# Linear attention and a GEGLU feed-forward on one core: both weight halves in one tile, one norm on two engines, one sum of h placed later

## The chip, the core and the metric

The kernel runs on one core of a Trainium2 chip. A core has TensorE (PE, matmuls), VectorE (DVE), ScalarE (ACT), GpSimd (POOL) and a queue (SP) that issues DMAs. Each engine works through its own instructions in the order in which the program lists them, and engines wait for each other on semaphores. The metric is the device time of one execution in microseconds; lower is better.

## The reference

Eight batches of 576 tokens with 8 heads of 64. The attention is linear: queries are normalized over the head dimension, keys over the tokens. Its output, 4608 tokens by 512, goes through a gated feed-forward of width 1536.

```python
q_s = np.exp(q - max(q, -1)); q_s = q_s / (sum(q_s, -1) + 1e-09)
k_s = np.exp(k - max(k, 2));  k_s = k_s / (sum(k_s, 2) + 1e-09)
kv = np.einsum('bhsd,bhse->bhde', k_s, v)
attn = np.einsum('bhsd,bhde->bhse', q_s, kv)
x = attn.transpose(0, 2, 1, 3).reshape(B * S, H * D)
out = (gelu(x @ w_gate) * (x @ w_val)) @ w_out
```

Inputs and output are float32; the kernel works in float16 with float32 sums.

## The kernel before

**Batches.** The loop at L1023 goes over batches 0 to 6, then 8, then 7. Batches 0 to 7 are the 512 main tokens of each batch; "batch 8" gathers the remaining 64 tokens of all eight. While the feed-forward of one batch runs on TensorE, the attention of the next is prepared: `exp` (L208, ScalarE), `norm_sum` (L226, VectorE: row sums and reciprocal), `norm_mul` (L248, VectorE or GpSimd: the exponentials, called eq, times the reciprocals), a transpose (`unit_t` on TensorE in batches 0 and 1, `unit_td` by DMA later), `unit_kv` and `unit_x`, which gives xt, the input of the feed-forward.

**Feed-forward.** Its width is cut into 12 tiles of 128 (fi). Batches 0 and 1 take each tile with plain matmuls into psg and psv (L467), then Gelu on ScalarE (L472) and the product on VectorE (L473), which gives ht. Batches 2 and later use a Winograd form of Strassen's scheme: 7 block products in place of 8. For that they need sums of blocks:

- sums of the weights: `sum_wgv` (L591), four for gate (g) and four for value (v), on pairs of tiles k and k+3. Sum 1 is a21+a22, sum 2 is sum 1 - a11, sum 3 is a11-a21 written over a21 in the weight tile itself, sum 4 is a12 - sum 2. For k = 0 to 2 they are made in batch 0, three k in one operation; for k = 6, 7, 8 each k by itself, and gate and value each by itself: 128x256 elements an operation. Where these results lie is set by `w_sum` (L586), `wst16` (L553) and the views `ws` at L121 to L123.
- sums of x: `sum_x` (L600), on GpSimd.
- sums of h for the output product: `sum_h` (L572), four for each pair of tiles: sums 1 and 2 on VectorE, 3 and 4 mostly on GpSimd in batches 2 and 3. `sum_w` (L558) makes the sums of w_out.

**Order.** It is written by hand. In batches 2 and later the strings at L621 to L626 list the steps: "k.i" is step i of the pair k (`pair_step`), "8g" and "8v" are plain halves of tile 8 (`half`), and other words stand for work planned under that name. FOUR serves batches 2 and 3. Its "s1" plans the first and third sum of h of pair 1 (tiles 1 and 4, with 7 and 10), "u1" the second and fourth; "u1" is called in the output stage. In step 3 of a pair, `upper` (L660) makes the upper half of ht: Gelu on ScalarE, then a product on GpSimd (L663).

The table `plan`, filled by `at(b, kind, i, ...)`, hangs other work onto the places of the program: FI after a tile of batches 0 and 1, NS in the output stage. The last norm of batch 1 (head pair 3) hangs at (0, NS, 16) at L948 and runs on VectorE; the next place, (0, NS, 17), has sum_w(3) and sum_w(2) on GpSimd. The transposes that need the norm are the first thing in batch 1 (L953, `unit_t`).

**Output stage.** `out_strassen` (L742) runs product 1 (psa), 2 (psb), 5 (psc), 6 (psa), 3 (psc), 7 (psa) and 4 (psa), six tiles each. In between, VectorE or ScalarE takes snapshots (L762, L764) of psa and psc, and VectorE adds bank and snapshot into the output tile yo (L770). Product 3 adds into psc and so comes after psc's snapshot; product 4 overwrites psa and so comes after the add of psa. The place (b, NS, 2) lies between psa's second snapshot and that add.

Of the kernel before, what the change touches and what calls it, by code (L numbers as in the profile page):

```python
# [9 lines left out]
f32 = mybir.dt.float32  # L10
f16 = mybir.dt.float16
ACTF = mybir.ActivationFunctionType
ALU = mybir.AluOpType
# [5 lines left out]
def kernel(  # L19
# [10 lines left out]
    nc = tc.nc  # L30

    B, H, S, D = q.shape
    C = H * D
    F = moe_w_gate.shape[1]
    P = 128
    HP = H // 2
# [12 lines left out]
    NO = NFI // 2  # L49

    const = ctx.enter_context(tc.tile_pool(name="const", bufs=1))
    wpool = ctx.enter_context(tc.tile_pool(name="wpool", bufs=1))
# [52 lines left out]
    ek_b, eq_b, v16_b = [], [], []  # L105
# [7 lines left out]
    ws = {(nm, 0): const.tile([P, 3, 2, NO // 2 * P], f16, name=f"ws{nm}") for nm in "gv"}  # L113
# [4 lines left out]


    kt1 = ld_b["k"][1].rearrange("p h x -> p (h x)").bitcast(f16)  # L120
    for i, nm in enumerate("gv"):  # L121
        n = 3 * NO * P
        ws[(nm, 1)] = kt1[:, i * n:(i + 1) * n].rearrange("p (s c f) -> p s c f", s=3, c=2)  # L123
    cc_b = [x.rearrange("p n c -> p (n c)").bitcast(f32)[:, 0:1024].rearrange(
        "p (i t r) -> p i t r", i=2, t=2) for x in eq_b]

# [1 line left out]
        "p (i c r) -> p i c r", i=4, c=2)]  # L128

    q0r = [x[0:64].rearrange("p (h d) -> p h d", d=D) for x in (  # L130
        kt1[:, 2 * n:].bitcast(f32), eq_b[1].rearrange("p n c -> p (n c)").bitcast(f32)[:, 1024:])]

    def buf(bs, b):
        return bs[b % len(bs) if b < 4 else 0]
# [10 lines left out]
    nc.gpsimd.memset(v16_b[0][:, :, :, D:D + 1], 1.0)  # L145
    nc.gpsimd.memset(ld_b["k"][1][:, :, 0:D], -1e30)

    wg_sb = wpool.tile([P, HP, F], f16, name="wg_sb")
    wv_sb = wpool.tile([P, HP, F], f16, name="wv_sb")
    wo_sb = wpool.tile([P, NFI, C], f16, name="wo_sb")  # L150


# [82 lines left out]
    def norm_pair(b, g, n0, engs):  # L235

        n = NC - n0
        e = buf(eq_b, b)[:, n0:NC, 2 * g * P:(2 * g + 2) * P].rearrange("p n (h d) -> p n h d", d=D)
        rq = att.tile([P, n, 4], f32, name="rq2", tag="rq2", bufs=2)
        nc.vector.reduce_sum(rq, e, axis=mybir.AxisListType.X)  # L240
        rrq = att.tile([P, n, 4], f32, name="rrq2", tag="rrq2", bufs=2)
        nc.vector.reciprocal(out=rrq, in_=rq)  # L242
        for j in range(2):
            st[(b, "norm", 2 * g + j)] = (e[:, :, 2 * j:2 * j + 2], rrq[:, :, 2 * j:2 * j + 2], n)
        for j, eng in enumerate(engs):
            norm_mul(b, 2 * g + j, eng)

    def norm_mul(b, hp, eng="dve"):  # L248
        e, rrq, n = st[(b, "norm", hp)]
        (nc.gpsimd if eng == "pool" else nc.vector).tensor_tensor(  # L250
            out=e, in0=e, in1=rrq.unsqueeze(-1).to_broadcast((P, n, 2, D)), op=ALU.mult)

    def norm(b, hp, eng="dve", n0=0):
        norm_sum(b, hp, n0)
        norm_mul(b, hp, eng)
# [21 lines left out]
    st = {}  # L277
# [272 lines left out]
    tw, ws67 = {}, {}  # L550


    def wst16(name, key):  # L553
        t = wstp.tile([P, NO * 256 + 512], f16, name=name, tag="wst")
        ws67[key] = t[:, NO * 256:].rearrange("p (c f) -> p c f", c=2)
        return t[:, 0:NO * 256].rearrange("p (j c) -> p j c", j=NO)

    def sum_w(i, eng="dve"):  # L558
        t = wst16(f"tw{i}", (None, ("g", 0), ("v", 0), ("g", 1), ("v", 1))[i])
        b11, b12 = wo_sb[:, 0:NO, 0:256], wo_sb[:, 0:NO, 256:512]  # L560
        b21, b22 = wo_sb[:, NO:NFI, 0:256], wo_sb[:, NO:NFI, 256:512]
        a, b = {1: (b12, b11), 2: (b22, tw.get(1)), 3: (b22, b12), 4: (b21, tw.get(2))}[i]
        (nc.gpsimd if eng == "pool" else nc.vector).tensor_tensor(out=t, in0=a, in1=b, op=ALU.subtract)
        tw[i] = t

    sh = {}

    def make_s():
        for i in (1, 2):
            sh[i] = wst16(f"sh{i}", (None, ("g", 2), ("v", 2))[i])  # L570

    def sum_h(j0, j1, which, eng="dve"):  # L572
        step = 1 if j0 in (0, 4) and j1 < NO + (j0 > 0) else NO // 2
# [9 lines left out]

    def w_sum(nm, j, k, n=1):  # L586
        if k in (NO, NO + 1):
            return ws67[(nm, j)][:, :, (k - NO) * P:(k - NO + n) * P]
        return ws[(nm, k // NO)][:, j, :, k % NO * P:(k % NO + n) * P]

    def sum_wgv(nm, i, k=0, n=NO // 2, eng="dve"):  # L591
        w = wg_sb if nm == "g" else wv_sb
        lo, hi = slice(k * P, (k + n) * P), slice((k + NO // 2) * P, (k + NO // 2 + n) * P)
        a11, a21, a12, a22 = w[:, 0:2, lo], w[:, 0:2, hi], w[:, 2:4, lo], w[:, 2:4, hi]
        t = [w_sum(nm, j, k, n) for j in range(3)]
        o, a, b, op = {1: (t[0], a21, a22, ALU.add), 2: (t[1], t[0], a11, ALU.subtract),
                       3: (a21, a11, a21, ALU.subtract), 4: (t[2], a12, t[1], ALU.subtract)}[i]
        (nc.gpsimd if eng == "pool" else nc.vector).tensor_tensor(out=o, in0=a, in1=b, op=op)  # L598
# [7 lines left out]
    def product_gv(i, ps, xt, k, first):  # L606
        lo, hi = slice(k * P, (k + 1) * P), slice((k + NO // 2) * P, (k + NO // 2 + 1) * P)
        xs = xs_b[xt is st.get((B - 1, "xt"))]
        for t, w, nm in ((0, wv_sb, "v"), (1, wg_sb, "g")):
            for c in range(2):  # L610
                a = {1: w[:, c, lo], 2: w[:, 2 + c, lo], 4: w[:, 2 + c, hi], 7: w[:, c, hi]}.get(i)
                if a is None:
                    a = w_sum(nm, {3: 2, 5: 0, 6: 1}[i], k)[:, c]
                x = {1: xt[:, c, 0:256], 2: xt[:, 2 + c, 0:256], 3: xt[:, 2 + c, 256:512],
                     4: xs[:, 3, c], 5: xs[:, 0, c], 6: xs[:, 1, c], 7: xs[:, 2, c]}[i]
                nc.tensor.matmul(ps[:, t], a, x, start=(first and t == 0 and c == 0), stop=(c == 1),  # L616
                                 skip_group_check=True)
# [1 line left out]


    FOUR = ("a 7g l 7v n 0.1 6.1 0.2 6.2 0.3 6.3 m p 10g 0.4 6.4 1.1 t 10v 1.2 s0 8g u0 1.3 8v 1.4 2.1"  # L621
            " 11g s1 2.2 11v 2.3")
    FIVE = ("a 8g l 8v n m 0.1 6.1 0.2 6.2 0.3 6.3 0.4 1.1 p 6.4 7.1 t 1.2 7.2 1.3 s0 7.3 2.1 1.4 u0 11g 2.2"
            " y 7.4 11v 2.3 s1")
    SIX = ("0.1 6.1 0.2 6.2 0.3 6.3 0.4 1.1 6.4 7.1 s0 1.2 7.2 1.3 u0 7.3 1.4 2.1 7.4 8.1 2.2"
# [306 lines left out]
    FI, NS, PR = range(3)  # L932
    plan = {}

    def at(b, kind, i, *fns):
        plan.setdefault((b, kind, i), []).extend(fns)

    L = lambda f, *a: (lambda: f(*a))

    def load_2nd():  # L940
        load_batch(2, ((q, "q"), (k, "k")))

    at(0, FI, NFI - 1, L(exp, "q", 1, 0, 4), L(exp, "q", 1, 4, 8), load_2nd, L(exp, "k", 1, 0, 4),
       L(cast_w_o, 3), L(cast_w_o, 4), L(cast_w_o, 5),
       L(norm, 1, 0), L(norm, 1, 1), L(norm_sum, 1, 2), L(norm_mul, 1, 2, "pool"),
       L(cast_v, 1, 0, 4, "act"), L(exp, "k", 1, 4, 8))
    at(0, NS, 5, L(unit_t, 1, 0))
    at(0, NS, 16, L(unit_kv, 1, 0), L(cast_v, 1, 4, 8), L(load_batch, 2, ((v, "v"),)),  # L948
       L(norm, 1, 3))
    at(0, NS, 17, L(unit_x, 1, 0, "act", True), L(unit_x, 1, 1, "act", True), L(sum_w, 3, "pool"),  # L950
       L(sum_w, 2, "pool"))
    at(0, NS, 7, L(exp, "q", 2))
    first1 = [[L(unit_t, 1, 1), L(unit_kv, 1, 1)],  # L953
# [10 lines left out]
    at(1, FI, 2, L(unit_trem, 1))  # L964
    at(1, FI, 3, L(norm, 2, 2, "pool"), L(load_batch, 3, ((q, "q"), (k, "k"))))
    at(1, FI, 4, L(exp, "k", 2, 0, 4), L(norm, 2, 3, "pool"), L(sum_w, 4), make_s)
    at(1, FI, 5, L(cast_v, 2, 0, H))
    at(1, FI, 8, L(unit_td, 2))
# [5 lines left out]
    for i, x in enumerate(("g1", "v1", "g2", "v2", "g4", "v4")):  # L974
        at(0, FI, 5 + i, L(sum_wgv, x[0], int(x[1])))
    at(0, FI, NFI - 2, L(sum_w, 1))
    at(1, NS, 1, L(sum_wgv, "g", 3))
    at(1, NS, 2, L(sum_wgv, "v", 3))
    for b in range(2, B):
        n = b + 1  # L980
# [14 lines left out]
    for b in range(2, B - 1):  # L995
        n = b + 1
# [6 lines left out]
    for b in range(2, B + 1):  # L1003
        for j in range(NO // 2 - 1):
# [3 lines left out]
            else:  # L1008
                at(b, PR, f"s{j}", L(sum_h, j, NO, (3,), "pool"))
                at(b, PR, f"u{j}", L(sum_h, j, NO, (2,)), L(sum_h, j, NO, (4,), "pool"))  # L1010
    for b, i, kind, dk, xs_ in (
            (1, 6, FI, 0, ("g1", "v1", "g2", "v2", "g4", "v4")), (1, 9, FI, 0, ("g3", "v3")),
            (2, 1, NS, 1, ("g1", "v1", "g2", "v2")), (3, 2, NS, 1, ("g4", "v4", "g3", "v3")),
            (4, 2, NS, 2, ("g1", "v1", "g2", "v2")), (6, 1, NS, 2, ("g4", "v4")), (6, 2, NS, 2, ("g3", "v3"))):
        for x in xs_:
            at(b, kind, i, L(sum_wgv, x[0], int(x[1]), NO + dk, 1, "pool" if b < 3 else "dve"))


    def ride(b, kind, i):
# [3 lines left out]
    for b in order:  # L1023
# [16 lines left out]
        if b == 0:  # L1040
# [5 lines left out]
            for ns in range(4):  # L1046
                cut = 9 if ns == 2 else 7 if ns == 3 else NFI
# [37 lines left out]
```

## Time and profile before

| What | us |
|---|---|
| median of 3 runs | 294.36 (294.34 to 294.36) |
| the profiled execution | 298.55 |
| its span, first to last instruction | 296.8 |

Busy time in that execution:

| Engine | us |
|---|---|
| PE | 282.7 |
| DVE | 232.5 |
| POOL | 200.0 |
| ACT | 198.4 |

The mean granted TensorE clock is 0.991 of full speed. The lines of the profile in the prediction give a start in us from the span's first instruction, a length in us, the engine, the line of the code, the operation, "out<-in" by the program's names with shapes, and a count; a bracket at the end is the engine's idle time just before, with what ended it. Lines that stand for several instructions ("x4") are merged.

### The profile page before, as it was taken

The numbers are of one execution on the slowest core, as the hardware profiler recorded it, in microseconds if no ns is written. First come the engines' busy times: TensorE is split into PE (matmuls) and PEld (weight loads), VectorE is DVE, ScalarE is ACT, GpSimd is POOL, SyncE is SP. The second block draws the span as 40 slices with busy tenths as digits, with TensorE's granted clock in tenths as the row PEclk, the third lists the DMA queues.
The fourth block names the chain that finished last, engine by engine and source line by source line (L and its number), as shares of the span: only waits on it lengthen the run. The fifth ranks groups of instructions, "written<-read, shape, count | busy, mean of one in ns | idle before, by whom it ended". The sixth has DMA issues, their size and how long they took to land.

```text
span 296.8 us, 6506 instructions
## 1 busy us (share of the span) xinstructions
PE 282.7 (95%) x2497; PEld 208.5 (70%) x2497; DVE 232.5 (78%) x432; ACT 198.4 (67%) x332; POOL 200.0 (67%) x189
## 2 busy tenths in 40 slices
PE   3899997999999999999899999999999999999994
PEld 1444444544877686868688877888788888888883
DVE  2855889786997787768997989887988879938982
ACT  3763377374788669866977697769775477537650
POOL 1567548469278869995797589668976476293640
PEclk9999999799999999999999999999999999999998
DMA  6999999978119901990099208930332110033003
GB/s 222 372 380 390 400 390 393 342 282 190 58 75 353 285 3 71 331 301 9 23 328 334 44 3 305 334 71 2 141 58 45 71 74 0 3 71 73 2 0 141
DMA packets 54622, 51.72 MB, mean 174 GB/s; under 512 B 18496, under 2 KB 50496, under 8 KB 54592
## 3 DMA queue, kind: packets, MB, share of 16 engines
q1 hardware_dynamic: 52864, 49.49, 51.8%
q10 hardware_dynamic: 1728, 1.84, 1.9%
q8 instruction: 19, 0.31, 0.4%
q14 instruction: 11, 0.09, 0.1%
HBM read 37.75 MB, written 9.44 MB: 159 GB/s over the span
## 4 chain that ended last, share of the span: by engine, by line
PE 88%; DVE 6%; DMA 2%; issue 1%; ACT 1%; POOL 1%; POOLq 0%; ACTq 0%
PE pga L616 21%; PE psa L732 14%; PE psg L467 11%; PE psv L467 11%; PE pgc L616 10%; PE psc L732 6%; PE pgb L616 5%; PE psb L732 4%; PE psy L535 3%; DMA qt<-in_q_dram 2%; PE pskv L343 2%; DVE eq L250 1%; DVE kt L598 1%; PE pst L368 1%; PE psx L430 1%
## 5 line engine op out<-in xcount | busy, mean ns | idle before, releaser
L250 POOL TENSOR_TENSOR eq<-eq,rrq 128x640 f16<-128x640 f16 (+1 forms) x27 | 34.7, 1303 | 16.6 <-DVE rrq L242 8.4
L732 PEld LDWEIGHTS <-ht 128*128 128x128 f16 x384 | 36.8, 98 | 8.8 <-issue 4.0
L467 PE MATMUL psg<-xt,wg_sb 128*128 128x512 f16 x152 | 41.6, 383 | 0.0
L467 PE MATMUL psv<-xt,wv_sb 128*128 128x512 f16 x152 | 41.4, 382 | 0.0
L663 POOL TENSOR_TENSOR ht<-eq 128x512 f16<-128x512 f32 x17 | 21.6, 1273 | 19.2 <-ACT eq L661 19.2
L616 PEld LDWEIGHTS <-wv_sb 128*128 128x128 f16 x280 | 27.0, 98 | 8.0 <-issue 0.8
L616 PEld LDWEIGHTS <-wg_sb 128*128 128x128 f16 x280 | 27.4, 98 | 3.2
L582 POOL TENSOR_TENSOR s<-ht,sh 128x512 f16<-128x512 f16 x16 | 18.7, 1169 | 14.5 <-DVE sh L582 14.5
L472 ACT ACTIVATE gl<-psg 128x512 f32<-128x512 f32 x24 | 13.8, 597 | 21.2 <-PE psg L467 21.2
L643 ACT ACTIVATE glq<-pgb 128x256 f32<-128x256 f32 x35 | 13.3, 381 | 21.1 <-PE pgb L616 14.4
L644 DVE SCALAR_TENSOR_TENSOR ht<-pga,glq 128x256 f16<-128x256 f32 x35 | 14.8, 422 | 14.9 <-ACT glq L643 14.6
L467 PEld LDWEIGHTS <-wv_sb 128*128 128x128 f16 x152 | 14.9, 98 | 16.3 <-issue 1.2
L582 POOL TENSOR_TENSOR ht<-ht 128x512 f16<-128x512 f16 x16 | 19.0, 1188 | 10.0 <-DVE sh L582 10.0
L467 PEld LDWEIGHTS <-wg_sb 128*128 128x128 f16 x152 | 15.0, 99 | 14.8 <-issue 0.6
L732 PE MATMUL psa<-tw,ht 128*128 128x256 f16 x192 | 23.4, 272 | 1.6 <-DVE yo L770 1.5
L673 ACT COPY pgb<-pga 128x512 f32<-128x512 f32 x35 | 20.4, 582 | 6.1 <-PE pga L616 5.8
L473 DVE SCALAR_TENSOR_TENSOR ht<-psv,gl 128x512 f16<-128x512 f32 x24 | 16.0, 685 | 9.3 <-PE psv L467 7.3
L653 ACT ACTIVATE snq<-pga 128x512 f32<-128x512 f32 x35 | 20.9, 600 | 3.5 <-PE pga L616 3.2
L188 POOL CAST v<-vt 128x640 f16<-128x640 f32 x26 | 18.7, 760 | 6.7 <-PE pskv L343 5.4
L663 POOL TENSOR_TENSOR ht<-cc 128x512 f16<-128x512 f32 x16 | 20.3, 1271 | 3.0 <-ACT cc L661 3.0
L616 PE MATMUL pga<-xs,wv_sb 128*128 128x256 f16 x116 | 22.1, 272 | 0.2 <-DVE cc L657 0.2
L212 ACT ACTIVATE ek<-kt 128x1280 f16<-128x1280 f32 (+1 forms) x11 | 19.1, 1748 | 4.8 <-DMA kt<-in_k_dram 3.3
(182 smaller groups left out, 761.9 us busy)
## 6 DMA issues: line engine op xcount, KB each, us to landing
out_dram<-yo SPq DMA_DIRECT2D x15, 512.0 KB, 3.4
kt<-in_k_dram SPq DMA_DIRECT2D x7, 640.0 KB, 8.3
vt<-in_v_dram SPq DMA_DIRECT2D x7, 640.0 KB, 5.5
qt<-in_q_dram SPq DMA_DIRECT2D x7, 640.0 KB, 6.7
qt<-in_q_dram SPq DMA_DIRECT2D x8, 512.0 KB, 7.1
wost<-in_moe_w_out_dram SPq DMA_DIRECT2D x6, 512.0 KB, 7.9
kt<-in_k_dram SPq DMA_DIRECT2D x6, 512.0 KB, 9.2
vt<-in_v_dram SPq DMA_DIRECT2D x6, 512.0 KB, 6.0
```

Of the source, the lines that this page charges most:

```text
L188: nc.gpsimd.tensor_copy(out=dst, in_=src)
L212: nc.scalar.activation(out=dst[:, n0:NC, h0 * D:h1 * D].rearrange(o, d=D, **({"t": 2} if b >= QUAD else {})), in_=heads(tiles[(nm, b)], b, ...
L250: (nc.gpsimd if eng == "pool" else nc.vector).tensor_tensor(out=e, in0=e, in1=rrq.unsqueeze(-1).to_broadcast((P, n, 2, D)), op=ALU.mult)
L467: nc.tensor.matmul(ps, w[:, ci, fi * P:(fi + 1) * P], xt[:, ci, :], start=(ci == 0), stop=(ci == HP - 1))
L473: nc.vector.scalar_tensor_tensor(out=ht[:, fi, :], in0=psv, scalar=_H_SCALE, in1=gl, op0=ALU.mult, op1=ALU.mult)
L582: (nc.gpsimd if eng == "pool" else nc.vector).tensor_tensor(out=o, in0=a, in1=b, op=op)
L616: nc.tensor.matmul(ps[:, t], a, x, start=(first and t == 0 and c == 0), stop=(c == 1), skip_group_check=True)
L644: nc.vector.scalar_tensor_tensor(out=ht[:, fi, 0:256], in0=ps[:, 0], scalar=_H_SCALE, in1=gl, op0=ALU.mult, op1=ALU.mult)
L653: nc.scalar.activation(out=sn, in_=ps, func=ACTF.Copy, scale=_H_SCALE)
L663: (nc.vector if k == NFI - NO // 2 - 1 else nc.gpsimd).tensor_tensor(out=ht[:, k:k + NO // 2 + 1:NO // 2, 256:512], in0=cc[:, :, 0], in1=c ...
L673: nc.scalar.copy(out=pb, in_=pa)
L732: nc.tensor.matmul(ps[t], a, w, start=(first and j == js[0] and (t == ts[0] or ps[t].tensor is not ps[ts[0]].tensor)), stop=(j == js[-1]), ...
```

## The change

Four edits:

1. The weights of gate and value lie in one tile, wgv_sb, instead of two; wg_sb and wv_sb are views of its halves.
2. For k = 6, 7, 8 a sum is made for both weights by one operation (`sum_w1`) of 128x512 elements. The results lie with gate and value side by side: in `ws67` for k = 6, 7 and in `ws8`, a view of the second key buffer, for k = 8. The places in the plan stay the same: GpSimd in batches 1 and 2, VectorE in batches 3, 4 and 6.
3. The last norm of batch 1 is multiplied on two engines: rows 0 to 2 of 5 on VectorE, rows 3 and 4 on GpSimd.
4. In FOUR, "s1" moves from behind "11g" to the end of the list, behind "2.3".

```diff
-    for i, nm in enumerate("gv"):
-        n = 3 * NO * P
-        ws[(nm, 1)] = kt1[:, i * n:(i + 1) * n].rearrange("p (s c f) -> p s c f", s=3, c=2)
+    ws8 = kt1[:, 0:12 * P].rearrange("p (s w c f) -> p s w c f", s=3, w=2, c=2)
...
-    wg_sb = wpool.tile([P, HP, F], f16, name="wg_sb")
-    wv_sb = wpool.tile([P, HP, F], f16, name="wv_sb")
+    wgv_sb = wpool.tile([P, 2, HP, F], f16, name="wgv_sb")
+    wg_sb, wv_sb = wgv_sb[:, 0], wgv_sb[:, 1]
...
+    def norm_mul2(b, hp, cut):
+        e, rrq, n = st[(b, "norm", hp)]
+        for eng, r in ((nc.vector, slice(0, cut)), (nc.gpsimd, slice(cut, n))):
+            eng.tensor_tensor(out=e[:, r], in0=e[:, r], in1=rrq[:, r].unsqueeze(-1).to_broadcast(
+                (P, r.stop - r.start, 2, D)), op=ALU.mult)
...
-        ws67[key] = t[:, NO * 256:].rearrange("p (c f) -> p c f", c=2)
+        ws67[key] = t[:, NO * 256:].rearrange("p (w c f) -> p w c f", w=2, c=2)
...
-        t = wst16(f"tw{i}", (None, ("g", 0), ("v", 0), ("g", 1), ("v", 1))[i])
+        t = wst16(f"tw{i}", (None, (NO, 0), (NO, 1), (NO, 2), (NO + 1, 0))[i])
...
+    def sum_w1(i, k, eng):
+        lo, hi = slice(k * P, (k + 1) * P), slice((k + NO // 2) * P, (k + NO // 2 + 1) * P)
+        a11, a21, a12 = wgv_sb[:, :, 0:2, lo], wgv_sb[:, :, 0:2, hi], wgv_sb[:, :, 2:4, lo]
+        a22 = wgv_sb[:, :, 2:4, hi]
+        t = [ws8[:, j] if k == NO + 2 else ws67[(k, j)] for j in range(3)]
         o, a, b, op = {1: (t[0], a21, a22, ALU.add), 2: (t[1], t[0], a11, ALU.subtract),
                        3: (a21, a11, a21, ALU.subtract), 4: (t[2], a12, t[1], ALU.subtract)}[i]
         (nc.gpsimd if eng == "pool" else nc.vector).tensor_tensor(out=o, in0=a, in1=b, op=op)
...
-            " 11g s1 2.2 11v 2.3")
+            " 11g 2.2 11v 2.3 s1")
...
-       L(norm, 1, 3))
+       L(norm_sum, 1, 3), L(norm_mul2, 1, 3, 3))
...
-    for b, i, kind, dk, xs_ in (
-            (1, 6, FI, 0, ("g1", "v1", "g2", "v2", "g4", "v4")), (1, 9, FI, 0, ("g3", "v3")),
-            (2, 1, NS, 1, ("g1", "v1", "g2", "v2")), (3, 2, NS, 1, ("g4", "v4", "g3", "v3")),
-            (4, 2, NS, 2, ("g1", "v1", "g2", "v2")), (6, 1, NS, 2, ("g4", "v4")), (6, 2, NS, 2, ("g3", "v3"))):
-        for x in xs_:
-            at(b, kind, i, L(sum_wgv, x[0], int(x[1]), NO + dk, 1, "pool" if b < 3 else "dve"))
+    for b, kind, i, dk, x in ((1, FI, 6, 0, 1), (1, FI, 6, 0, 2), (1, FI, 6, 0, 4), (1, FI, 9, 0, 3),
+                              (2, NS, 1, 1, 1), (2, NS, 1, 1, 2), (3, NS, 2, 1, 4), (3, NS, 2, 1, 3),
+                              (4, NS, 2, 2, 1), (4, NS, 2, 2, 2), (6, NS, 1, 2, 4), (6, NS, 2, 2, 3)):
+        at(b, kind, i, L(sum_w1, x, NO + dk, "pool" if b < 3 else "dve"))
```

More of the change, by code (lines that the diff above doesn't have):

```diff
@@ L130 @@
     q0r = [x[0:64].rearrange("p (h d) -> p h d", d=D) for x in (
-        kt1[:, 2 * n:].bitcast(f32), eq_b[1].rearrange("p n c -> p (n c)").bitcast(f32)[:, 1024:])]
+        kt1[:, 36 * P:].bitcast(f32), eq_b[1].rearrange("p n c -> p (n c)").bitcast(f32)[:, 1024:])]
     def buf(bs, b):
@@ L569, in make_s @@
         for i in (1, 2):
-            sh[i] = wst16(f"sh{i}", (None, ("g", 2), ("v", 2))[i])
+            sh[i] = wst16(f"sh{i}", (None, (NO + 1, 1), (NO + 1, 2))[i])
     def sum_h(j0, j1, which, eng="dve"):
@@ L582, in sum_h, with w_sum @@
             (nc.gpsimd if eng == "pool" else nc.vector).tensor_tensor(out=o, in0=a, in1=b, op=op)
[L586 to L589, printed above, removed]
+    def w_sum(nm, j, k):
+        if k < NO:
+            return ws[(nm, 0)][:, j, :, k * P:(k + 1) * P]
+        return (ws8[:, j] if k == NO + 2 else ws67[(k, j)])[:, "gv".index(nm)]
     def sum_wgv(nm, i, k=0, n=NO // 2, eng="dve"):
@@ L594, in sum_wgv @@
         a11, a21, a12, a22 = w[:, 0:2, lo], w[:, 0:2, hi], w[:, 2:4, lo], w[:, 2:4, hi]
-        t = [w_sum(nm, j, k, n) for j in range(3)]
+        t = [ws[(nm, 0)][:, j, :, k * P:(k + n) * P] for j in range(3)]
+        o, a, b, op = {1: (t[0], a21, a22, ALU.add), 2: (t[1], t[0], a11, ALU.subtract),
+                       3: (a21, a11, a21, ALU.subtract), 4: (t[2], a12, t[1], ALU.subtract)}[i]
+        (nc.gpsimd if eng == "pool" else nc.vector).tensor_tensor(out=o, in0=a, in1=b, op=op)
+    def sum_w1(i, k, eng):
[3 more added lines that the diff above has]
+        t = [ws8[:, j] if k == NO + 2 else ws67[(k, j)] for j in range(3)]
         o, a, b, op = {1: (t[0], a21, a22, ALU.add), 2: (t[1], t[0], a11, ALU.subtract),
```

## The prediction

> **What bounds the kernel now.** I read the page first, then the waits of TensorE, then the timeline around each wait.
>
> ```profile
> PE 282.7 (95%) x2497; PEld 208.5 (70%) x2497; DVE 232.5 (78%) x432; ACT 198.4 (67%) x332; POOL 200.0 (67%) x189
> ...
> PE 88%; DVE 6%; DMA 2%; issue 1%; ACT 1%; POOL 1%; POOLq 0%; ACTq 0%
> ```
>
> TensorE is busy 95% of the span and carries 88% of the chain of waits. No matmul is added or removed, so the time can change only through TensorE's gaps. The list of its waits has two entries that concern the edited code (total us, times, longest):
>
> ```profile
> PE pst L368 <- DVE eq L250: 2.7, 2, 2.1
> PE psa L732 <- DVE yo L770: 1.5, 2, 0.9
> ```
>
> The first one's large gap, in the timeline at the start of batch 1 (start, length, engine, instruction):
>
> ```profile
> 48.58 3.65 DVE L250 TENSOR_TENSOR eq<-eq,rrq 128x640 f16<-128x640 f16 x1
> ...
> 48.45 3.10 POOL L563 TENSOR_TENSOR tw<-wo_sb 128x1536 f16<-128x1536 f16 x1
> 51.51 3.67 POOL L563 TENSOR_TENSOR tw<-wo_sb,tw 128x1536 f16<-128x1536 f16 x1
> ...
> 52.28 0.48 PE L368 MATMUL pst<-ident,eq 128*128 128x128 f16 x4 [2.10 <-DVE eq L250]
> ```
>
> VectorE's norm multiply of batch 1 (head pair 3) takes 3.65 us; the same shape took 0.83 at 40.77 and 42.61. It was ready 0.13 us after GpSimd had begun sum_w(3), and it ended 0.7 us after that operation's end at 51.55. TensorE's four transposes wait 2.10 us for it.
>
> The second wait, output stage of batch 3, where four weight sums ride on VectorE:
>
> ```profile
> 142.67 0.68 DVE L598 TENSOR_TENSOR sh<-wg_sb,tw 128x256 f16<-128x256 f16 x1
> 143.28 0.80 DVE L598 TENSOR_TENSOR sh<-wv_sb,tw 128x256 f16<-128x256 f16 x1
> 144.00 0.80 DVE L598 TENSOR_TENSOR wg_sb<-wg_sb 128x256 f16<-128x256 f16 x1
> 144.72 0.80 DVE L598 TENSOR_TENSOR wv_sb<-wv_sb 128x256 f16<-128x256 f16 x1
> 145.45 0.68 DVE L770 SCALAR_TENSOR_TENSOR yo<-psa,sn 128x512 f32<-128x512 f32 x1
> ...
> 142.49 2.89 POOL L188 CAST v<-vt 128x640 f16<-128x640 f32 x4
> ...
> 146.18 1.47 PE L732 MATMUL psa<-tw,ht 128*128 128x256 f16 x12 [0.91 <-DVE yo L770]
> ```
>
> Undisturbed, such a sum takes 0.28 us (232.90). Here the four follow each other at 0.72 us, the pace of the four casts on GpSimd: one sum gets through per cast. L770 behind them is late and product 4 waits 0.91 us. Batch 4 has the same picture at 173.27 to 175.83 and a gap of 0.62 us at 176.49.
>
> For the moved sum I read the output stage of batch 2:
>
> ```profile
> 107.66 0.41 DVE L582 TENSOR_TENSOR sh<-sh,ht 128x512 f16<-128x512 f16 x1
> 108.00 0.42 DVE L582 TENSOR_TENSOR sh<-ht 128x512 f16<-128x512 f16 x1
> 108.45 1.26 DVE L582 TENSOR_TENSOR sh<-sh,ht 128x512 f16<-128x512 f16 x1
> ...
> 110.26 0.69 DVE L764 TENSOR_SCALAR sn<-psc 128x512 f32<-128x512 f32 x1
> ...
> 108.16 1.27 POOL L582 TENSOR_TENSOR s<-ht,sh 128x512 f16<-128x512 f16 x1 [0.64 <-DVE sh L582]
> ...
> 111.37 1.25 PE L732 MATMUL psc<-wo_sb,s 128*128 128x256 f16 x10
> ```
>
> The sum at 108.45 waits for GpSimd's end at 109.43. The snapshot of psc then ends at 110.95, and product 3, which adds into psc, starts at 111.37: 0.42 us of slack.
>
> [...] operations with a PSUM input (L657, L637, L770) keep 0.68 us beside busy GpSimd. [...] the trace has 1.16 (L604) and is used.
>
> **The change part by part.**
>
> *Norm split.* Removed: one VectorE multiply of 640 elements a partition. Added: one of 3 rows (384) on VectorE, one of 2 rows (256) on GpSimd ahead of sum_w(3) and sum_w(2). VectorE's multiply costs 0.69 at 512 and 0.83 at 640, so 384 is 0.56. GpSimd's costs 1.26 at 640, so 256 is about 0.55. GpSimd's casts end at 48.49, the reciprocal at 48.55. At 9.59 and 9.71, the same pair of a reciprocal's readers, VectorE starts 0.12 us first and GpSimd is held up. So: VectorE 48.58 to 49.14, GpSimd until about 49.75; in the other order the end is the same. TensorE is there at 50.2 and finds the rows ready: **-2.1 us**. What is late next: psy's evacuation behind the multiply on VectorE comes earlier by 3 us, ScalarE's exp and table load end at 53.92 where Gelu would start at 56.5, and sum_w ends about 56 while GpSimd's next norm can start at 56.8. So nothing takes the gap's place, and queries 3 (needed at 77.46) have long landed. Bounds: 0 if the parts still end after 52, -2.1 if covered; I take all of it.
>
> *Merged weight sums on VectorE, batches 3, 4, 6.* Four operations of 256 become two of 512 (0.41 undisturbed, L582). In batch 3 two casts are waited for instead of four: the second ends about 144.5 instead of 145.52. L770 then waits for product 7 (about 144.45) and ends at 145.2; TensorE comes to product 4 at 145.27: **-0.9 us**. In batch 4 likewise, second sum by 174.6, product 7 by 175.0, product 4 ready at 175.87: **-0.6 us**. ScalarE is full from 169.41 to 179.5 in batch 4 and doesn't move up; it has 0.7 us idle at 180.24 to catch up. In batch 6 VectorE idles 0.59 us for product 3 behind the sums: nothing.
>
> *Merged on GpSimd, batches 1 and 2.* Two of 0.67 become one of 1.16, 0.18 us less for each pair. Batch 2: two pairs, -0.35 us in a queue without pause up to 129. Batch 1: GpSimd idles for 5.4 us before 80.79, so its saving is free; but VectorE's sums of h at 72.58 and 73.86 now meet operations of 1.16 us instead of 0.66. [...] **+0.1**, bounds -0.2 and +0.6.
>
> *s1 later, batches 2 and 3.* VectorE's sum 1 moves from 102.91, where VectorE then still waits 0.22 us for ScalarE, to an idle place at 105.85: nothing gained or lost. GpSimd's sum 3 moves from a pause (103.40) to behind the upper part of step 2.3, 107.47 to 108.62. There it meets u1's sum 2 on VectorE (107.66), which ends at 108.9 instead of 108.07. All behind it on VectorE (both last sums, L770, the snapshot of psc) is 0.83 late; slack is 0.42, so product 3 loses **0.45 us in each of two batches**. GpSimd's queue is 0.9 late, less 0.35 in batch 2; sum_x at 117.18, for which TensorE's pgc at 118.39 already waits 0.17 us, loses **0.1** more against TensorE. Bounds for each batch: 0 [...], 1.2 if GpSimd wins each time.
>
> *Layout (one tile for both weights).* Same bytes and matmuls: nothing.
>
> Sum: -2.1 - 0.9 - 0.6 + 0.1 + 0.9 + 0.1 = -2.5 us of a span of 296.8 (298.55 us with what lies around it). The median is 294.36, 1.4% less, so the difference stays 2.5: **291.9**.
>
> **Rivals.** (B) The moved sum meets nobody: without its +1.0 the time is 290.9. For: the order of a few tenths decides. Against: sum 3 follows the upper part without a pause. (C) The norm gap goes, but in batches 3 and 4 ScalarE or GpSimd's sum_x takes over from L770, and s1 costs its 1.1: 294.36 - 2.1 + 1.1 = 293.4. For: ScalarE's full queue. Against: its idle 0.70 us just after. (D) The one weight tile makes matmuls of tile 10 in batch 1 wait for the in-place sum 3 on GpSimd, ending about 74.3 where they start at 71.58: +2.7, giving 294.6. Against: in before the same two-block write at 73.24 doesn't stop them. (E) Slower: a sum over both weights, with three levels of stride, costs GpSimd twice, 2.3 us. In batch 1 VectorE's sums of h then wait for such operations and L473 of tile 11 comes 3.9 late; in batch 2 sum_x comes 2.1 late: 294.36 - 2.5 + 5.9 = 297.8. It decides from about 1.65 us an operation. Against: L250 has three levels as well and runs at 1.26 for 640.
>
> **How the numbers follow.** Forecast 0.51, B 0.20, C 0.14, D 0.06, E 0.09. A measurement tells 0.2% (0.6 us) from no change. A, B and nearly all of C are faster: 0.83. D and C's edge are same: 0.07. E and D's edge are slower: 0.10. The range takes A, B and C with their bounds: 290.4 to 293.7.
>
> **What would show it.** Right: no gap at the transposes of batch 1, L250 on VectorE at 0.6 us, no wait of product 4 in batches 3 and 4, a new short gap ahead of product 3 in batches 2 and 3 with a snapshot of psc late. Wrong: L250 still over 2 us, POOL L250 parts started after sum_w, or merged sums over 1.5 us.

## The result and the profile after

| | before | after |
|---|---|---|
| median of the runs, us | 294.36 (294.34 to 294.37, 4 runs) | 294.31 (294.14 to 294.48, 4 runs) |
| profiled execution, us | 298.55 | 294.14 |
| its span, us | 296.8 | 292.1 |

The ratio after to before is 0.9998, 95% interval 0.9981 to 1.0016: no difference that can be told. The two profiled executions differ by 4.4 us all the same. The whole case lies in that contradiction.

The page of the changed kernel: busy shares, granted clock by slice, the chain that ended last.

```profile
PE 281.8 (96%) x2497; PEld 207.5 (71%) x2497; DVE 229.2 (78%) x426; ACT 198.1 (68%) x332; POOL 200.2 (69%) x184
...
PEclk9999999999999999999999999999999999999999
...
PE 87%; DVE 4%; POOL 4%; DMA 2%; ACT 1%; issue 1%; POOLq 0%; ACTq 0%
```

VectorE has 6 operations less and GpSimd 5. The clock row has no 7 in it (before had one in the eighth slice), and GpSimd has gone from 1% to 4% of the chain.

TensorE's waits of the changed kernel (total us, times, longest):

```profile
PE psc L745 <- POOL s L586: 0.5, 2, 0.3
PE pgc L629 <- POOL xs L617: 0.3, 1, 0.3
...
PE psb L745 <- DVE ht L477: 0.2, 1, 0.2
```

Both waits that the prediction wanted gone are gone: the 2.1 us at the transposes and the 1.5 us ahead of product 4. Three short ones have come: product 3 for GpSimd's sum of h, a weight-block product for the sum of x, and product 2 in batch 1 for the last tile of h.

The norm of batch 1 in the changed kernel's timeline (start, length, engine, instruction):

```profile
48.21 0.95 DVE L254 TENSOR_TENSOR eq<-eq,rrq 128x384 f16<-128x384 f16 x1
...
48.71 0.92 POOL L254 TENSOR_TENSOR eq<-eq,rrq 128x256 f16<-128x256 f16 x1
49.60 3.10 POOL L567 TENSOR_TENSOR tw<-wo_sb 128x1536 f16<-128x1536 f16 x1
...
49.42 0.61 PE L372 MATMUL pst<-ident,eq 128*128 128x128 f16 x8
```

The split does what was said of it: both parts end before 49.7, GpSimd's w_out sum comes behind them, and the eight transposes run without a gap.

To see where time goes when starts differ by some tenths between executions, I take the length of each batch on TensorE, from the start of product 2 of one output stage to the start of product 2 of the next (worked out from TensorE's timelines; the first column is the time of the first product 2, that of batch 1):

```
                      first  1-2    2-3    3-4    4-5    5-6    6-8    8-7
before, first profile 76.35  31.09  30.50  30.59  30.31  29.62  28.59  27.62
before, run again     72.32  31.10  30.48  30.59  30.31  29.62  28.58  27.62
norm split alone      72.18  31.10  30.49  30.58  30.31  29.62  28.58  27.62
merged sums alone     72.33  31.45  30.32  29.63  29.63  29.62  28.58  27.62
s1 later alone        72.18  31.10  31.32  30.77  30.30  29.62  28.58  27.62
after, s1 put back    72.35  31.54  30.33  29.63  29.64  29.63  28.59  27.62
after                 72.04  31.56  31.19  30.05  29.62  29.63  28.58  27.63
merged, sum 3 moved   72.20  31.11  30.34  29.63  29.64  29.63  28.58  27.63
```

The columns repeat to 0.02 us where nothing is changed, so a difference of a tenth can be read. Against the second row, the changed kernel loses 0.46 in batch 1-2 and 0.71 in 2-3 and wins 0.54 in 3-4 and 0.69 in 4-5. And the first profile of before stands 4 us apart from all other rows, in the first column only.

### The profile page after: what moved, and what is told of

Its sections match the earlier page's. It is cut to its first block, busy times and chain, and to the rows that moved or that the text cites. A ratio compares the mean times of both kernels' runs of the same rounds, so it can differ in the third digit from the quotient of the medians.

```text
span 292.1 us, 6496 instructions
## 1 busy us (share of the span) xinstructions
PE 281.8 (96%) x2497; PEld 207.5 (71%) x2497; DVE 229.2 (78%) x426; ACT 198.1 (68%) x332; POOL 200.2 (69%) x184
## 4 chain that ended last, share of the span: by engine, by line
PE 87%; DVE 4%; POOL 4%; DMA 2%; ACT 1%; issue 1%; POOLq 0%; ACTq 0%
PE pga L629 21%; PE psa L745 12%; PE psg L471 11%; PE psv L471 10%; PE pgc L629 10%; PE psc L745 6%; PE pgb L629 5%; PE psy L539 4%; PE psb L745 2%; DMA qt<-in_q_dram 2%; DVE sh L586 2%; PE pskv L347 2%; POOL s L586 1%; POOL v L186 1%; PE psx L434 1%
## 5 line engine op out<-in xcount | busy, mean ns | idle before, releaser
L629 PEld LDWEIGHTS <-wgv_sb 128*128 128x128 f16 x560 | 54.3, 98 | 11.2 <-issue 0.8
L471 PEld LDWEIGHTS <-wgv_sb 128*128 128x128 f16 x304 | 29.5, 98 | 30.3 <-issue 0.7
L471 PE MATMUL psg<-xt,wgv_sb 128*128 128x512 f16 x152 | 41.1, 379 | 0.0
L471 PE MATMUL psv<-xt,wgv_sb 128*128 128x512 f16 x152 | 41.0, 379 | 0.0
L629 PE MATMUL pga<-xs,wgv_sb 128*128 128x256 f16 x232 | 34.5, 272 | 0.2 <-DVE cc L670 0.2
L238 DVE TENSOR_REDUCE rq<-eq 128x20 f32<-128x1280 f16 (+1 forms) x12 | 17.2, 1432 | 4.4 <-ACT eq L210 4.4
L745 PEld LDWEIGHTS <-sh 128*128 128x128 f16 x192 | 18.7, 98 | 2.3
```

What stands on the lines that cost most here:

```text
L471: nc.tensor.matmul(ps, w[:, ci, fi * P:(fi + 1) * P], xt[:, ci, :], start=(ci == 0), stop=(ci == HP - 1))
L745: nc.tensor.matmul(ps[t], a, w, start=(first and j == js[0] and (t == ts[0] or ps[t].tensor is not ps[ts[0]].tensor)), stop=(j == js[-1]), ...
```

## Experiments

### The kernel before, once more

No edit.

> The kernel before, unchanged. Theory 1 (the wait of the transposes was a feature of the one profiled execution, 298.55 us, and not of the others): median 294.4, span about 292.3, clock 1.0, VectorE's norm multiply of batch 1 takes 0.8 to 1.5 us, TensorE waits for it under 0.5 us. Theory 2 (the wait is in every execution and the norm split earned its 2.1 us, which the other edits lost again): the multiply takes about 3.6 us again and TensorE waits about 2 us.

Measured: 294.38 us (294.19 to 297.11, 22 runs), ratio 1.0005 [0.9996, 1.0014]; the profiled execution took 294.5. Its timeline at the same place:

```profile
48.48 0.94 DVE L250 TENSOR_TENSOR eq<-eq,rrq 128x640 f16<-128x640 f16 x1
...
47.37 1.38 POOL L188 CAST v<-vt 128x640 f16<-128x640 f32 x2 [1.57 <-PE psy L535]
48.71 3.68 POOL L563 TENSOR_TENSOR tw<-wo_sb 128x1536 f16<-128x1536 f16 x1
...
49.70 0.61 PE L368 MATMUL pst<-ident,eq 128*128 128x128 f16 x8
```

The multiply takes 0.94 us, not 3.65, and no gap follows. In this execution GpSimd's casts began 0.26 us later (47.37, not 47.11), so the w_out sum came at 48.71, after the multiply had asked at 48.48. In the first profile it was there at 48.45, and the multiply asked 0.13 us too late, at 48.58. Now it is the w_out sum that is stretched (3.68 in place of 3.10), which nobody waits for. In each of the two executions the instruction that starts second takes longer than it does where it starts first; why is not shown. ("Asks" stands for the start that the profile gives an instruction.) The wait on which the largest term of the prediction rests wasn't there in an ordinary execution. Four runs below keep this multiply as it is (merged sums alone, s1 later alone, one more GpSimd instruction, sum 3 moved). In their traces VectorE asks 0.21 to 0.51 us before the w_out sum begins, and the multiply takes 0.88 to 1.23 us. None of the five has the gap.

### One part at a time

**The norm split alone:**

```diff
-       L(norm, 1, 3))
+       L(norm_sum, 1, 3), L(norm_mul2, 1, 3, 3))
```

> Only the norm is split, all else as before. Theory 1: nothing to earn in ordinary executions, 294.1 to 294.4. Theory 2: 292.3, 2.1 us faster.

Measured: 294.89 us (294.72 to 295.21, 14 runs), ratio 1.0020 [1.0012, 1.0028]. Its row in the table is that of before: the split wins nothing here. Nor does it lose on TensorE; the half microsecond lies behind the last matmul. From the modelled end of TensorE's work to the end of the execution it takes 6.35 us here and 5.83 in before run again.

**The merged sums alone** (the changed kernel with the norm and the string FOUR of before):

```diff
-       L(norm_sum, 1, 3), L(norm_mul2, 1, 3, 3))
+       L(norm, 1, 3))
...
-            " 11g 2.2 11v 2.3 s1")
+            " 11g s1 2.2 11v 2.3")
```

> Only one tile for both weights and one operation for both weight sums. Theory 1: the waits of product 4 in batches 3 and 4 go (0.9 and 0.6 us), GpSimd's queue in batch 2 is 0.35 us shorter, and the longer operations cost some 0.4 us at the end of batch 1: about 1.2 us faster, 293.2. Theory 2: [...] 1 us or more slower: 295.4.

Measured: 292.89 us (292.67 to 293.05, 5 runs), ratio 0.9950 [0.9938, 0.9962]. Batch 3's output stage in its timeline:

```profile
138.84 0.82 DVE L611 TENSOR_TENSOR sh<-wgv_sb,sh 128x512 f16<-128x512 f16 x1
139.58 0.93 DVE L611 TENSOR_TENSOR wgv_sb<-wgv_sb 128x512 f16<-128x512 f16 x1
140.63 0.69 DVE L783 SCALAR_TENSOR_TENSOR yo<-psa,sn 128x512 f32<-128x512 f32 x1
```

Two sums take 1.67 us where four took 2.85, beside GpSimd's four casts of v, which run from 138.66 to 141.76 here. The add of psa behind the sums comes early enough: product 4 has no wait left here nor in batch 4. From the table: 3-4 is 0.96 shorter, 4-5 is 0.68 shorter, 2-3 is 0.16 shorter, and 1-2 is 0.35 longer. The sum is -1.45; the medians say -1.47.

**s1 later alone:**

```diff
-            " 11g s1 2.2 11v 2.3")
+            " 11g 2.2 11v 2.3 s1")
```

> Only s1 is moved behind 2.3. Theory 1: product 3 of batches 2 and 3 waits 0.3 to 0.5 us each and sum_x of batch 3 some tenths: 0.9 us slower, 295.2. Theory 2: 1 us slower as well or more. If neither holds and the move is hidden, 294.4.

Measured: 295.37 us (295.26 to 295.57, 5 runs), ratio 1.0036 [1.0024, 1.0048]. GpSimd in the output stage of batch 2, first in before run again:

```profile
99.37 1.16 POOL L582 TENSOR_TENSOR ht<-ht 128x512 f16<-128x512 f16 x1 [0.65 <-DVE sh L582]
102.22 1.27 POOL L663 TENSOR_TENSOR ht<-eq 128x512 f16<-128x512 f32 x1 [1.69 <-ACT eq L661]
104.13 1.27 POOL L582 TENSOR_TENSOR s<-ht,sh 128x512 f16<-128x512 f16 x1 [0.64 <-DVE sh L582]
105.76 1.16 POOL L582 TENSOR_TENSOR s<-ht,sh 128x512 f16<-128x512 f16 x1 [0.36 <-DVE sh L582]
```

and then with s1 later, with TensorE's two waits below:

```profile
102.08 1.27 POOL L663 TENSOR_TENSOR ht<-eq 128x512 f16<-128x512 f32 x1 [3.50 <-ACT eq L661]
103.31 1.16 POOL L582 TENSOR_TENSOR ht<-ht 128x512 f16<-128x512 f16 x1
104.83 1.27 POOL L582 TENSOR_TENSOR s<-ht,sh 128x512 f16<-128x512 f16 x1 [0.36 <-DVE sh L582]
106.45 1.16 POOL L582 TENSOR_TENSOR s<-ht,sh 128x512 f16<-128x512 f16 x1 [0.36 <-DVE sh L582]
...
107.62 1.25 PE L732 MATMUL psc<-wo_sb,s 128*128 128x256 f16 x10 [0.26 <-POOL s L582]
115.06 0.38 PE L616 MATMUL pgc<-xs,wsv 128*128 128x256 f16 x2 [0.42 <-POOL xs L604]
```

The sum that filled a pause at 99.37 now stands at 103.31, behind `upper` without a pause. VectorE's next sum of h meets it there: it begins at 103.50 and takes 1.25 us (1.24 in the changed kernel's trace, at 103.83), where in before run again it took 0.41. So the two sums s that product 3 reads come 0.7 us later (106.45 for 105.76), and product 3 itself starts 4.34 us after product 2 in place of 3.93, which is 0.41 later. (The 0.26 in the bracket is less, since it counts from the modelled end of the matmuls before.) In batch 2 the sum of x behind them on GpSimd is late as well and costs TensorE another 0.42. Batch 2-3 is 0.84 longer, 3-4 only 0.18. There product 3 is late by 0.42 too, but product 4 had waited 0.9 us before and waits 0.7 here, so it starts only 0.17 later. The sum is +1.02; the medians say +1.0.

**The changed kernel with s1 put back:**

```diff
-            " 11g 2.2 11v 2.3 s1")
+            " 11g s1 2.2 11v 2.3")
```

> The changed kernel with s1 at its old place behind 11g. Theory (the edits add up, and s1 later is the loss): 1.0 us faster than the changed kernel's 294.31, so 293.3 at most and about 292.9, the time of the weight sums alone, if the norm split costs nothing here. Rival (s1 later is needed once the sums are merged): 294.3 or slower.

Measured: 292.86 us (292.83 to 293.20, 5 runs), ratio 0.9949 [0.9936, 0.9961]: the merged sums alone within 0.03, so beside them the norm split wins nothing. In the table it costs 0.09 in batch 1-2: GpSimd's in-place weight sum begins 0.11 later there (69.14 for 69.03), and product 2 of batch 1 waits 0.42 us for the last tile of h where the merged sums alone have 0.33. And s1 costs more in the changed kernel than alone: 294.31 - 292.86 = 1.45 by the medians, 0.86 + 0.42 = 1.28 by the table. Once product 4 has no wait, nothing in batch 3 covers the late product 3.

### The half microsecond of the norm split alone

The split adds one GpSimd instruction. One more GpSimd instruction that touches nothing on the way:

```diff
-       L(norm, 1, 3))
+       L(norm, 1, 3), L(nc.gpsimd.memset, tiny[:, 100:101], 0.0))
```

> The kernel before with one more small GpSimd operation (a memset of one column) behind the norm of batch 1, where GpSimd is idle. The norm split alone cost 0.5 us behind the last DMA issue, with all matmuls at the same times. Theory P (one more instruction in GpSimd's program costs it at the end): 294.9, with the tail behind the last issue 0.5 us longer. Theory Q (the split itself costs it): 294.4.

Measured: 294.45 us (294.29 to 294.76, 13 runs), ratio 0.9993 [0.9980, 1.0007]. One GpSimd instruction more is not the cause.

### When the multiply loses the race

**The norm's multiply 0.8 us later on VectorE,** behind an operation that empties the output bank psy:

```diff
-       L(norm, 1, 3))
+       L(norm_sum, 1, 3))
+    at(0, NS, 6, L(norm_mul, 1, 3))
```

> The kernel before with VectorE's norm multiply one operation (0.6 us) later, behind the evacuation of psy, so that sum_w(3) on GpSimd is always under way first. Theory [...]: the multiply takes 3 us or more in every execution, TensorE waits over 2 us for it, and the time is 296.8 to 298.5. Rival (the 298.55 us of the first profile had another cause): 294.4 to 295.

Measured: a median of 294.48 us (ratio 1.0012 [0.9988, 1.0037]), which says nothing, but two kinds of execution: 9 of 13 took 294.19 to 294.58 and 4 took 298.60 to 298.89. The profiled one is one of the four (298.78 us):

```profile
49.26 3.20 DVE L250 TENSOR_TENSOR eq<-eq,rrq 128x640 f16<-128x640 f16 x1
...
48.69 3.09 POOL L563 TENSOR_TENSOR tw<-wo_sb 128x1536 f16<-128x1536 f16 x1
...
52.52 0.61 PE L368 MATMUL pst<-ident,eq 128*128 128x128 f16 x4 [2.09 <-DVE eq L250]
```

It is the picture of the first profile: w_out sum first, multiply stretched, 2.09 us of gap. All batches after it have the lengths of before. Both of my cases missed: the multiply was to lose every time, or never. Whether it loses varies from execution to execution of one program. Why nine executions did not lose is not shown, as none of them left a trace. In the profiled one, 0.35 of the 0.78 us by which the multiply is later than in before run again is not the edit's: the reciprocals ahead of ours come at 48.58 in place of 48.23.

**Losing always.** The row sums and reciprocals of that norm are computed twice, so that the multiply asks after the w_out sum has begun:

```diff
-       L(norm, 1, 3))
+       L(norm_sum, 1, 3), L(norm, 1, 3))
```

> The kernel before with the row sums and reciprocals of batch 1's last norm computed twice, so that VectorE asks for its multiply 1.03 us later (about 49.5 us instead of 48.48), surely after GpSimd's 3.1 us wo addition has begun (48.71). Theory R ([...] whether the norm wait exists is decided by some tenths of a microsecond): now every execution loses, the multiply stretches to about 3 us, TensorE idles 2 to 3 us before the second four transposes and its clock dips after it: 298.4 to 299.2 in every execution, none near 294.4. Rival (the long executions have another cause and the multiply merely suffers with them): only the added 1.03 us counts, less the 0.35 us that the multiply was early: 294.9 to 295.2, with at most a few long ones.

Measured: 297.27 us (297.12 to 297.55, 5 runs), ratio 1.0103 [1.0089, 1.0117]. Now no execution is near 294.4.

```profile
49.26 3.20 DVE L250 TENSOR_TENSOR eq<-eq,rrq 128x640 f16<-128x640 f16 x1
...
48.69 3.09 POOL L563 TENSOR_TENSOR tw<-wo_sb 128x1536 f16<-128x1536 f16 x1
...
52.52 0.40 PE L368 MATMUL pst<-ident,eq 128*128 128x128 f16 x4 [2.58 <-DVE eq L250]
```

The loss every time is as expected, and the rival's 294.9 to 295.2 is out. The size is not: I had expected 298.4 and more. The gap is longer than in the first profile and yet the time is 1.3 us shorter. The clock tells why. Windows of the first profile of before (length, busy time of PE, PEld, DVE, ACT, POOL with counts, granted clock, DMA share, GB/s):

```profile
50.00:52.00 2.00, 0.18 (x4) 0.01 (x1) 2.00 (x1) 1.93 (x1) 2.00 (x2) 1.00 1.09 402
52.00:53.00 1.00, 0.72 (x9) 0.72 (x10) 1.00 (x3) 0.98 (x2) 1.00 (x1) 0.73 1.01 399
53.00:55.00 2.00, 2.00 (x12) 1.16 (x11) 1.28 (x4) 0.91 (x2) 2.00 (x1) 0.50 1.06 391
55.00:56.00 1.00, 1.00 (x4) 0.36 (x3) 0.00 (x0) 0.00 (x0) 0.17 (x1) 0.56 1.11 405
56.00:58.00 2.00, 2.00 (x11) 0.89 (x10) 1.58 (x3) 0.00 (x0) 0.00 (x0) 1.00 1.33 306
```

and two of the same windows where the sums are made twice:

```profile
52.00:53.00 1.00, 0.48 (x9) 0.49 (x10) 1.00 (x3) 0.98 (x2) 1.00 (x1) 1.00 1.01 401
53.00:55.00 2.00, 2.00 (x17) 1.03 (x15) 1.74 (x6) 1.12 (x2) 2.00 (x1) 1.00 1.06 391
```

In the first profile TensorE runs at half clock (0.50) behind the gap, and with the sums made twice it does not (1.00). Taking these two for the only values, the means 0.73, 0.50 (over 2 us) and 0.56 give as an estimate 0.54 + 2 + 0.88 = 3.42 us at half clock, worth 1.71 us of full clock. With the gap of 2.10 that is 3.81 of the 4.19 us between the profiled execution and the median. Half clock followed 2.10 us of gap in the first profile and did not follow 2.58 us in this run, so a gap's length alone doesn't decide. What does decide is not shown.

The late multiply's profile has the same dip: means of 0.75, 0.50 (over 2 us) and 0.54 in the same windows, which by the same estimate is 3.42 us at half clock again. The mean clock recorded with each run tells the two sizes apart. The four long executions of the late multiply have 0.992 to 0.994, and the five here 0.997 to 1.000, which fits the wait without the half clock; no short execution has less than 0.996.

**The same with the multiply split:**

```diff
-       L(norm, 1, 3))
+       L(norm_sum, 1, 3), L(norm_sum, 1, 3), L(norm_mul2, 1, 3, 3))
```

> The same, with the multiply then split over VectorE and GpSimd as the change does. Theory R: GpSimd's part stands ahead of its wo addition, so the addition can't begin before the norm is done, and the lost wait can't occur: the 1.03 us of added sums remain on the path, 295.0 to 295.8 in every execution, some 3 us under the run without the split. If instead the split saves only length (3 of 5 tiles), the difference between the two is under 1 us.

Measured: 294.52 us (294.38 to 294.78, 13 runs), ratio 1.0009 [1.0000, 1.0017]: 2.75 us under the run without the split.

```profile
49.17 0.56 DVE L256 TENSOR_TENSOR eq<-eq,rrq 128x384 f16<-128x384 f16 x1
...
49.22 0.98 POOL L256 TENSOR_TENSOR eq<-eq,rrq 128x256 f16<-128x256 f16 x1 [0.64 <-DVE rrq L232]
50.17 3.09 POOL L569 TENSOR_TENSOR tw<-wo_sb 128x1536 f16<-128x1536 f16 x1
...
50.26 0.29 PE L374 MATMUL pst<-ident,eq 128*128 128x128 f16 x2 [0.19 <-POOL eq L256]
```

GpSimd's own part keeps the w_out sum back to 50.17, and 0.19 us of wait is left. The time is below my 295.0 to 295.8: I had put most of the added 1.03 us on the path, but TensorE's last matmul ends only 0.29 us later than in before run again (288.96 for 288.67), and what follows it is shorter here, 5.56 us in place of 5.83. The split is worth 2.75 us where the race is lost, and where it is won it takes nothing off TensorE's time.

### Without either collision

The merged sums alone, with GpSimd's in-place sum 3 of batch 1 behind the casts of v in the output stage:

```diff
-    for b, kind, i, dk, x in ((1, FI, 6, 0, 1), (1, FI, 6, 0, 2), (1, FI, 6, 0, 4), (1, FI, 9, 0, 3),
+    for b, kind, i, dk, x in ((1, FI, 6, 0, 1), (1, FI, 6, 0, 2), (1, FI, 6, 0, 4), (1, NS, 2, 0, 3),
```

> Merged weight sums alone (292.89), with sum 3 of k=6 on GpSimd moved from behind tile 9 of batch 1 to behind the casts of v in the output stage, away from VectorE's sums of h. Theory [...]: 292.5, L473 of tile 11 0.3 us earlier and no wait of product 2. Rival: 292.9.

Measured: 292.44 us (292.15 to 292.70, 5 runs), ratio 0.9926 [0.9913, 0.9940]. The end of batch 1, first with the merged sums alone:

```profile
69.65 1.53 DVE L586 TENSOR_TENSOR sh<-sh,ht 128x1024 f16<-128x1024 f16 x1
...
72.90 0.68 DVE L477 SCALAR_TENSOR_TENSOR ht<-psv,gl 128x512 f16<-128x512 f32 x1
...
69.03 1.60 POOL L611 TENSOR_TENSOR wgv_sb<-wgv_sb 128x512 f16<-128x512 f16 x1
```

and with sum 3 moved:

```profile
69.52 0.69 DVE L586 TENSOR_TENSOR sh<-sh,ht 128x1024 f16<-128x1024 f16 x1
...
71.93 0.68 DVE L477 SCALAR_TENSOR_TENSOR ht<-psv,gl 128x512 f16<-128x512 f32 x1
...
79.65 1.15 POOL L611 TENSOR_TENSOR wgv_sb<-wgv_sb 128x512 f16<-128x512 f16 x1
```

VectorE's sum of h falls from 1.53 to 0.69 us and the product for tile 11 comes 0.97 earlier (0.84 when counted from product 2); batch 1-2 is back at 31.11. So the 0.35 us that merging cost in batch 1 was this collision.

The norm split on top of that (the changed kernel with s1 put back and sum 3 moved, both edits as above):

> The changed kernel with the sum of h of pair 1 put back to its old place and GpSimd's weight sum 3 of batch 1 put behind the casts of v, that is the merged sums, the split norm, and neither collision. If the parts add up as so far: 292.4, the same as without the split within 0.2, and no execution above 293.2. If the split carries the half microsecond at the end of the kernel that it carried when it was alone: 292.9 to 293.0.

Measured: 292.50 us (292.43 to 292.67, 5 runs), ratio 0.9940 [0.9927, 0.9953]. The same within the measurement, and no half microsecond at the end: 5.87 us follow TensorE's last matmul. Of the two, this is the version to keep. It beats both kernels by 1.8 us. Its order leaves the norm no race against the w_out sum: none of the 41 executions with a split norm was a long one. At 3 in 99 about one long one would be expected among 41, so it is the 13 with the sums made twice, against 5 of 5 lost, that show it.

## Why the prediction was wrong

The forecast was -2.5 us; the medians give -0.05. Term by term, as the prediction put them:

| term | predicted | measured |
|---|---|---|
| norm split | -2.1 | 0 alone (no column of the table moves), +0.09 beside the merged sums |
| merged sums, batch 3 | -0.9 | -0.96 |
| merged sums, batch 4 | -0.6 | -0.68 |
| merged sums, batch 2 | a shorter queue | -0.16 |
| merged sums, batch 1 | +0.1 | +0.35 |
| s1 later | +1.0 | +1.28 (alone +1.02) |
| sum | -2.5 | -0.08 by these terms, -0.05 by the medians |

**The step that failed** is the end of the sum: "The median is 294.36, 1.4% less, so the difference stays 2.5". It took the 4.2 us between the profiled execution and the median for a difference in scale. They were the norm wait itself and the half clock behind it: 2.10 + 1.71 = 3.81 of the 4.19. The race was read rightly from the profile (multiply against w_out sum, 0.13 us too late), and the split removes it, as losing always with and without it shows. But the 2.1 us were already absent from the time of 294.36 to which they were applied. Nor does time change "only through TensorE's gaps", as the prediction has it at its start: 1.71 us of the difference were TensorE's clock, by the estimate above. Of 99 further executions of the kernel before, 96 took 294.15 to 294.75 and 3 took 296.98, 297.11 and 298.99. That these three lost the race fits their times and their mean clocks (1.000, 0.998 and 0.992: two with the wait alone, one with half clock behind it), but none of them left a profile. The first one, at 298.55, did.

The profile had given the hint: the prediction notes that VectorE was 0.13 us late, and a wait that hangs on 0.13 us between two engines can be absent, as it was in before run again, where the multiply asked 0.23 us ahead of the w_out sum. Rivals B and C took the full gap as well; D and E reached 294.6 and above by way of events that did not occur (no matmul of tile 10 waits for sum 3, and a merged sum takes GpSimd 1.15 us, not 2.3). So the true time, which is the median less only what the other edits bring, was nobody's case; D's 294.6 lies near the measured 294.31 by luck.

**Right:** the merged sums on VectorE, to within 0.08 us in both batches; the pair of operations gets past GpSimd's casts in 1.67 us, where the four took 2.85. Right too is what s1 does to product 3: it starts 0.42 us later in each of the two batches, where I had 0.45, and by the collision that was named. The late snapshot of psc ends at 107.57 in the run of s1 alone, and GpSimd's s, to which the wait is put down, 0.04 us behind it. **Mis-sized:** batch 1, where +0.1 was an estimate of mine from operations of 1.16 us (GpSimd's 128x512 sums of x, L604 in the first profile). The one that collides, the in-place sum 3, begins at 69.03 and lasts 1.60 beside VectorE's sum; +0.35 is within the bound of 0.6 that was given. And the sum of x in batch 2, to which I gave 0.1: it costs 0.43 in the changed kernel. In batch 3 gain and loss add there as predicted (-0.96 + 0.42 = -0.54, column 3-4). Measured alone, s1 shows less, because the wait ahead of product 4, which the merged sums remove, covers 0.25 of its 0.42.

**What stays open:** the half microsecond of the norm split alone, behind TensorE's last matmul. It isn't one GpSimd instruction more, and it isn't there when the split stands beside the merged sums, nor with the sums made twice. With the same work at the end, that stretch took 5.56 to 5.89 us in all other profiled executions and 6.35 in this one, with all 14 runs above 294.7. Open as well are why nine of thirteen executions with the late multiply did not lose, and what decides whether half clock follows the gap.

## What to carry to other kernels

Before an expected gain is taken from a profile, hold its execution against the runs: where it is some per cent longer, look for the wait that makes it so, since a wait of that size may be missing from the time to be improved. A wait that hangs on which of two engines asks first, by tenths of a microsecond, is worth its size times how often it is lost. An operation put ahead in the winner's own queue can settle the order: here it did in 13 of 13 executions. And when a change removes a wait, price the other edits anew: what that wait had covered is no longer free.

## What the runs showed of the hardware

- One race decided by some tenths of a microsecond (lost by 0.13 in the first profile, won by 0.21 to 0.51 in five other traces) makes an execution longer by 2.75 us (sums made twice, without and with the split) or by 4.3 (the two kinds of the late multiply), so that one program shows well-separated times on one core. The kernel before had 3 long executions in 99, the late multiply 4 in 13, the sums made twice 5 in 5.
- Of the norm's multiply and GpSimd's w_out sum, the one that started second took longer than where it started first. Both orders are seen here with the same two instructions: multiply 0.94 and w_out sum 3.68 when the multiply was first (before run again), or multiply 3.65 and w_out sum 3.10 when the w_out sum was first (first profile). What holds the second one up is not shown. Between two GpSimd operations without a pause, the waiting multiply got through when it had asked 0.23 us before the second one began (before run again).
- A TensorE gap of 2.1 us was followed by an estimated 3.4 us at half clock (granted clock 0.50) in two profiled executions (the first profile and the late multiply), and a gap of 2.58 us by none in a third (1.00, sums made twice).
